# Attention and a two-layer network in one kernel: the last eight token blocks taken in pairs, with seven half-size products for the first layer

## The chip, the cores and the metric

The kernel runs on one core of a Trainium2 chip. Its engines are TensorE (matrix products, with separate weight loads), VectorE (DVE in the profile), ScalarE (ACT), GpSimd (POOL) and SyncE (SP), whose queue issues the transfers (DMA). TensorE writes its products into PSUM, eight banks of 512 float32 values on each of 128 partitions; VectorE and ScalarE read them from there. The metric is device time in microseconds of one execution, as the median of the runs.

## The reference

A linear attention is followed by a two-layer network over its output. For 8 batches and 8 heads, with 576 positions of 64 values and 128 features:

```
proj = x @ w_phi;  proj -= max(abs(proj), last axis)
phi(x) = concat(exp(proj), exp(-proj))              # 256 features, of q and of k
kv = phi(k)^T @ v;   z = sum over positions of phi(k)
attn = (phi(q) @ kv) / (phi(q) @ z + 1e-6)
x = attn as 4608 tokens of 512 values
h = x @ w_in                 # 512 -> 2048
out = gelu(h) @ w_out        # 2048 -> 512, gelu with erf
```

## The kernel before

Attention is worked batch by batch (`attention`, `k_quad`, `q_pair`, `quotients`): projections and sums on TensorE (tiles pk, kv, pq, pn), exponentials on ScalarE, maxima and denominators across partitions on GpSimd (mb, db). Numerators go to DRAM as x_d, reciprocal denominators as r_d. The 64-bit weights are turned into float32 once at the start (`split_weight`).

The network takes 18 blocks of 256 tokens. Every factor is held as two parts, the value rounded to TensorE's fast 32-bit form (float32r) and the remainder, and a product is three matmuls: high x high, high x low, low x high. `tokens` loads a block's numerators (xr) and reciprocals, multiplies and splits them (xh, xl). `up` computes a 128-feature part of the first layer into a PSUM tile ph, with 12 matmuls of 128 x 256 (four chunks of the 512 inputs, times three). Each block has eight units u with two such parts, so 192 matmuls.

Blocks 0 to 7 (`block`) run while attention is still under way: gelu on ScalarE, the remainder on VectorE, second layer into tile po with 96 matmuls of 128 x 512. Blocks 8 to 17 (`seven`) run after it. There the second layer of a unit is a 2 x 2 product of halves, in Strassen's way: seven products (m1 to m7) of sums of halves instead of eight, 21 matmuls of 128 x 256 into a four-bank tile pm. Sums of the activations (sg, oh, ol, uh, ul) are made on VectorE and ScalarE, sums of the second layer's weights once, during blocks 2 to 5 of the plan (`sums_of_weights`, tiles ts), stored in DRAM (t_d) and fetched back at block 8 into tw and over parts of w_o (`fetch_sums`). `turn_over` then closes attention's pools and reopens their space. Each later block is 192 + 168 = 360 matmuls of 256 columns.

The order of work is not written by hand. Each operation is recorded with engine, cost, rank, buffers and dependences (`Plan.op`); `Plan.order` runs a list schedule with these costs and ranks, a model of transfers among them, and `emit` writes every engine's instructions in that order. Engines, and SP's queue, then work strictly through their lists, and an instruction that waits holds up all behind it. The constants at the end of the file set ranks, delays (`since`) and lumps of attention work on TensorE (`LUMP`, `LINGER`). Line 329 is the helper `mm` for all matmuls, 364 to 370 are the helpers `copy` and `tt`, so groups are told apart by tiles.

## Time and profile before

| what | value |
|---|---|
| median of 3 runs (lowest to highest) | 1088.41 us (1087.9 to 1089.75) |
| the profiled execution | 1087.47 us |
| its span, first to last instruction | 1085.7 us |
| mean granted TensorE clock | 0.991 |
| moved by DMA | 106.05 MB |

The profile is of one execution. The page gives busy time by engine, the chain of work that ended last, and groups of instructions; other views give stretches of time, groups kept apart by shape, and every instruction in order. Matmuls overlap: a matmul of 256 columns is listed with some 0.28 us, and the next one starts 0.113 us after it. So the time of TensorE's work is read from starts, not from durations. The same holds on VectorE, where an instruction's duration overlaps the start of the next. In a row of a group, the last part is the idle time of the engine before these instructions and what ended it.

### The profile page before, as it was taken

The page shows a single profiled execution, that of the slowest core. Times are in us where ns is not written, and L with a number is a line of the kernel's source. Part 1 is how long each engine was busy: PE and PEld are TensorE (multiplying, and loading weights), DVE is VectorE, ACT ScalarE, POOL GpSimd, SP SyncE. Part 2 cuts the span into 40 slices and gives each one's busy share as a digit, 9 for nine tenths or more (in the row PEclk, how much of TensorE's full clock was granted, in tenths as well). Part 3 has the DMA queues.
Part 4 walks back from the last instruction along what each step waited for, and adds up shares of the span by engine and source line. Part 5 has one row for each costly group of instructions (what it writes and reads, how often), then busy time and mean ns, then how long its engine had stood idle before and what let it go on. Part 6 is the DMA issues. An engine that isn't in the chain of part 4 may idle for free.

```text
span 1085.7 us, 24204 instructions
## 1 busy us (share of the span) xinstructions
PE 1052.7 (97%) x9857; PEld 915.4 (84%) x9857; DVE 701.4 (65%) x1323; ACT 642.2 (59%) x1083; POOL 325.7 (30%) x116
## 2 busy tenths in 40 slices
PE   7879999999999999999999999999999999999996
PEld 4547858887877788877788888999999999999996
DVE  5888989467879997775653444465465465466444
ACT  5768786786767777766677683344344343344333
POOL 1321225754635755557655561000000000000000
PEclk8999999999999999999999999999999999999998
DMA  6887532224343343432321336421021021021000
GB/s 251 261 244 221 180 86 87 62 87 140 101 147 109 113 148 111 133 107 59 94 71 30 102 89 203 170 59 40 20 59 40 21 59 40 21 59 39 2 21 21
DMA packets 85216, 106.05 MB, mean 98 GB/s; under 512 B 24992, under 2 KB 66112, under 8 KB 85104
## 3 DMA queue, kind: packets, MB, share of 16 engines
q1 hardware_dynamic: 85104, 104.50, 31.6%
q8 instruction: 77, 1.26, 0.5%
q14 instruction: 35, 0.29, 0.1%
HBM read 74.81 MB, written 29.66 MB: 96 GB/s over the span
## 4 chain that ended last, share of the span: by engine, by line
PE 78%; DVE 11%; ACT 4%; DMA 3%; issue 2%; POOL 1%; SPq 0%; ACTq 0%; DVEq 0%; POOLq 0%
PE ph L329 33%; PE pm L329 18%; PE po L329 13%; PE kv L329 4%; PE pn L329 4%; PE pq L329 2%; PE pk L329 2%; DVE ts L370 2%; ACT ek L459 1%; DVE mx L454 1%; DVE ek L370 1%; DMA x_d<-xo 1%; DVE pc L370 1%; POOL db L537 1%; DVE un L531 1%
## 5 line engine op out<-in xcount | busy, mean ns | idle before, releaser
L329 PE MATMUL ph<-xh,w_i 128*128 128x256 f32 x2304 | 418.6, 278 | 1.1 <-ACT ga L714 0.7
L329 PEld LDWEIGHTS ph<-xh,w_i 128*128 128x128 f32 x2304 | 357.3, 188 | 8.2 <-issue 4.8
L329 PE MATMUL ph<-xl,w_i 128*128 128x256 f32 x1152 | 318.6, 277 | 0.0
L537 POOL PARTITION_ALL_REDUCE db<-un x48 | 182.1, 3793 | 159.7 <-DVE un L534 152.2
L329 PEld LDWEIGHTS ph<-xl,w_i 128*128 128x128 f32 x1152 | 216.4, 188 | 0.3
L502 POOL PARTITION_ALL_REDUCE mb<-pc x64 | 145.7, 2276 | 174.6 <-ACT pc L364 133.2
L370 DVE TENSOR_TENSOR sg<-ga 128x256 f32<-128x256 f32 (+1 forms) x240 | 84.5, 376 | 160.8 <-ACT ga L714 157.9
L329 PE MATMUL po<-w_o,gh 128*128 128x512 f32 (+1 forms) x520 | 164.8, 399 | 0.0
L714 ACT ACTIVATE ga<-ph 128x512 f32<-128x512 f32 x80 | 47.7, 597 | 165.6 <-PE ph L329 161.9
L329 PEld LDWEIGHTS po<-w_o,gh 128*128 128x128 f32 x520 | 92.5, 188 | 26.6 <-issue 4.7
L329 PE MATMUL pm<-w_o,oh 128*128 128x256 f32 x640 | 114.0, 277 | 0.0
L329 PEld LDWEIGHTS kv<-vt,ek 128*64 128x64 f32 (+1 forms) x2560 | 84.8, 140 | 27.2 <-issue 13.0
L329 PE MATMUL pn<-ef,kvn 128*64 128x288 f32 (+1 forms) x512 | 96.6, 422 | 7.9 <-ACT xo L364 7.7
L329 PE MATMUL po<-w_o,gl 128*128 128x512 f32 (+1 forms) x289 | 101.1, 368 | 0.4 <-DVE gl L370 0.4
L459 ACT ACTIVATE ek<-ek 128x1024 f32<-128x1024 f32 (+1 forms) x96 | 80.8, 843 | 32.7 <-DVE ek L370 31.6
L329 PEld LDWEIGHTS pm<-w_o,oh 128*128 128x128 f32 x640 | 96.5, 188 | 0.2 <-issue 0.2
L329 PE MATMUL kv<-vt,ek 128*64 128x65 f32 (+1 forms) x2560 | 93.7, 227 | 3.0 <-ACT ek L459 2.3
L508 ACT ACTIVATE ef<-pc 128x576 f32<-128x576 f32 x128 | 81.6, 678 | 14.7 <-DVE pc L370 14.2
L329 PE MATMUL pm<-w_o,ol 128*128 128x256 f32 x320 | 88.5, 277 | 0.0
L329 PE MATMUL pm<-tw,uh 128*128 128x256 f32 x480 | 86.0, 277 | 0.0
L370 DVE TENSOR_TENSOR pc<-pc,mb 128x576 f32<-128x576 f32 x64 | 50.9, 795 | 44.0 <-POOL mb L502 44.0
L370 DVE TENSOR_TENSOR gl<-ph,gh 128x512 fp32r<-128x512 f32 x64 | 43.8, 685 | 49.8 <-ACT ph L633 43.4
(63 smaller groups left out, 1549.7 us busy)
## 6 DMA issues: line engine op xcount, KB each, us to landing
t_d<-ts SPq DMA_DIRECT2D x40, 256.0 KB
vt<-in_va_dram SPq DMA_DIRECT2D x16, 585.0 KB
qt<-in_qT_dram SPq DMA_DIRECT2D x64, 144.0 KB
kt<-in_kT_dram SPq DMA_DIRECT2D x16, 576.0 KB
out_dram<-ob SPq DMA_DIRECT2D x36, 256.0 KB
raw_i<-in_w_in_dram SPq DMA_DIRECT2D x16, 512.0 KB
raw_o<-in_w_out_dram SPq DMA_DIRECT2D x16, 512.0 KB
x_d<-xo SPq DMA_DIRECT2D x48, 144.0 KB
```

Source lines behind the costliest of these rows:

```text
L329: return tc.keep_in_program_order(nc.tensor.matmul(*a, **kw))
L370: op(eng, cost, lambda: e.tensor_tensor(out=dst(), in0=a(), in1=b(), op=o), r=r, w=w, **kw)
L454: op("dve", dve(256 * n, True), lambda xs=xs, mx=mx: nc.vector.tensor_reduce(out=mx(), in_=xs(), axis=AX.X, op=ALU.max, apply_absolute_val ...
L459: op("act", act(256 * n), lambda e=e, s=s: nc.scalar.activation(e[s](), e[1](), AF.Exp, scale=1.0 - 2.0 * s), r=[e[1]], w=[e[s]], table="e ...
L502: op("pool", 2.2, lambda mb=mb, pc=pc: nc.gpsimd.partition_all_reduce(mb(), pc(), P, bass_isa.ReduceOp.absmax), r=[pc], w=[mb], port="max" ...
L508: op("act", act(2 * HS), lambda ef=ef, pc=pc, s=s: nc.scalar.activation(ef()[:, s], pc(), AF.Exp, scale=1.0 - 2.0 * s), r=[pc], w=[ef], ta ...
L531: op("dve", dve(HS, fast=True) + 0.06, lambda un=un, ef=ef, one=one, j=j: nc.vector.tensor_scalar(out=un()[:, j], in0=ef()[:, 0, j], scala ...
L537: op("pool", 3.7, lambda db=db, un=un: nc.gpsimd.partition_all_reduce(db(), un(), P, bass_isa.ReduceOp.add), r=[un], w=[db], port="add", * ...
L714: op("act", act(2 * TB, True) + 0.037, lambda ph=ph, ga=ga: nc.scalar.activation(ga(), ph(), AF.Gelu), r=[ph_all], w=[ga], table="gelu", **dr)
```

## The change

Blocks 8 and 9 stay single (`single`). Blocks 10 to 17 are taken two at a time (`pair`): the 512 tokens x 512 inputs of a pair and the weights of features u and u + 8 are each taken as 2 x 2 halves, and the first layer of a unit becomes seven products of half size (Winograd's form of Strassen's scheme), each of six matmuls of 128 x 256, instead of two blocks' 2 x 24 matmuls. Their sums of tokens (b11, t1 to t4, b21, b22) are formed once for a pair (`pair_tokens`); sums of w_in are formed during the early blocks, stored in DRAM (m_d) together with the plain parts, and read again for each pair through a ring of four slots (ri), which lie where the no longer needed w_in parts were. The seven products of a unit go in turn to the halves of two PSUM banks (ph twice, or h0 and h1), from where ScalarE and VectorE gather them: a running sum s, the first block's activations ga and the second block's gb. gb is kept until the first block's second layer is done (`seconds` runs first for block j, then for block j + 1). The running sum s and the first quarter of the result (c11) share space in a corner of former weights.

The second layer's accumulators, one tile pm of four banks before, become pa0, pa1 (one bank each) and pb; `results` and `single` combine them in another order.

Sums of weights are now made from whole values: high and low part are added once for each weight tile (`whole`), then sums and differences are formed, rounded and given their remainders (`rounded`). Before, each sum added both parts of both weights and then the two halves. The planner's constants are all different, and attention's pace is a constant of its own (`AT`). Shortened, the diff reads:

```diff
-    EARLIER = dict(kt=2, vt=2, mx=2, ek=2, kvn=4, un=1, db=1, qt=2, pc=2, mb=1, ef=2, xo=2, dc=2)
+    EARLIER = dict(kt=2, vt=2, mx=2, ek=2, kvn=4, un=1, db=1, qt=2, pc=2, mb=1, ef=2, xo=2, dc=2, wr=1, ws=1)
...
-    LATER = dict(ga=1, sg=1, uh=2, ul=2) | {f"tw{k}": 1 for k in range(NFC // 2)}
+    LATER = {f"tw{k}": 1 for k in range(NFC // 2)} | {f"xo{k}": 1 for k in range(3)} | dict(xe=1)
...
-        t: plan.pool(lambda: shared[1], t, n) for t, n in dict(pp=1, kv=1, pn=1, pm=1).items()}
+        t: plan.pool(lambda: shared[1], t, n) for t, n in dict(pp=1, kv=1, pn=1, pa0=1, pa1=1, h0=1, h1=1).items()}
...
+    def rounded(plain, src, rank, places):
+        kw = dict(rank=rank)
+        t = sb["ob"]([P, 2, HDM], F32R, f"ts_{next(rounds)}")
+        copy("act", act(HDM), lambda: t()[:, 1], plain, [src], [t], **kw)
+        tt("dve", dve(HDM), lambda: t()[:, 0], plain, lambda: t()[:, 1].bitcast(F32), ALU.subtract, [src, t], [t], **kw)
...
+    def whole(dst, buf, w, cols, n, rank):
+        tt("dve", dve(n), dst, lambda: w().bitcast(F32)[:, 0, cols], lambda: w().bitcast(F32)[:, 1, cols], ALU.add, [w], [buf], rank=rank)
...
-            for i, (x, xc, y, yc, o) in enumerate((
-                    (b, low_cols, a, high_cols, ALU.add), (b, low_cols, b, high_cols, ALU.add), (a, low_cols, a, high_cols, ALU.add),
-                    (b, high_cols, a, high_cols, ALU.subtract), (a, low_cols, b, low_cols, ALU.subtract))):
...
-                tt("dve", dve(2 * HDM), plain, lambda x=x, xc=xc: x().bitcast(F32)[:, :, xc], lambda y=y, yc=yc: y().bitcast(F32)[:, :, yc], o, [x, y], [t], **kw)
-                tt("dve", dve(HDM), lambda low=low: low().bitcast(F32), lambda low=low: low().bitcast(F32), lambda high=high: high().bitcast(F32), ALU.add, [t], [t], **kw)
-                copy("act", act(HDM), high, lambda low=low: low().bitcast(F32), [t], [t], **kw)
-                tt("dve", dve(HDM), low, lambda low=low: low().bitcast(F32), lambda high=high: high().bitcast(F32), ALU.subtract, [t], [t], **kw)
...
+            for i, w in enumerate((wo[k], wo[k + 8])):
+                whole(lambda raw=raw, i=i: raw()[:, 2 * i : 2 * i + 2].rearrange("p a t -> p (a t)"), raw, w, slice(0, DM), DM, rk)
...
+            for i, dst, buf, x, y, o in ((0, new(0), sum_, bl, ar, ALU.add), (1, new(1), sum_, bl, br, ALU.add), (3, br, raw, br, ar, ALU.subtract),
+                                         (2, ar, raw, al, ar, ALU.add), (4, al, raw, al, bl, ALU.subtract)):
+                tt("dve", dve(HDM), dst, x, y, o, [raw], [buf], rank=rk)
+                rounded(dst, buf, rk, [(d, lambda d=d, i=i: d()[:, i], lambda p: p)])
+        first = [Buf(plan, None, lambda e=e: dpool.tile([P, 2, 2, 2, P], F32, name=f"m_d{e}")) for e in range(7 * NFC // 4)]
...
+                    quarters = a11, a21, a12, a22 = wi[ci, q], wi[ci, q + 2], wi[2 + ci, q], wi[2 + ci, q + 2]
...
+                    for i, w in enumerate(quarters):
+                        whole(one(i), raw, w, cols, HDM, rk)
...
+                    for pos, dst, x, y, o in ((2, r22, r21, r22, ALU.add), (3, r21, r11, r21, ALU.subtract), (1, r11, r22, r11, ALU.subtract), (4, r12, r12, r11, ALU.subtract)):
+                        tt("dve", dve(HDM), dst, x, y, o, [raw], [raw], rank=rk)
...
+                        rounded(dst, raw, rk, places)
+                    for x, pos in ((a11, 0), (a22, 5), (a12, 6)):
...
+        xb = slot("w_i3_2", [P, NCC, TB], F32, f"xr_{j + 1}")
+        factor = slot("w_i0_2", [P, NCC, TB], F32, f"rb_{j}")
...
+        scaled_tokens(j, xa, factor, URGE + rank - SOON)
+        scaled_tokens(j + 1, xb, factor, URGE + rank - SOON)
+        half = lambda t, k: (lambda: t()[:, 2 * k : 2 * k + 2])
+        tt("dve", cost, half(factor, 0), half(xb, 1), half(xb, 0), ALU.subtract, [xb, factor], [factor], **soon)
+        tt("dve", cost, half(xb, 0), half(xb, 0), half(xa, 0), ALU.subtract, [xa, xb], [xb], **soon)
+        tt("dve", cost, half(factor, 1), half(xb, 1), half(xb, 0), ALU.subtract, [xb, factor], [factor], **soon)
+        X = {}
+        for k, tag, src, buf in (("b11", "xh", half(xa, 0), xa), ("t2", "xl", half(factor, 1), factor), ("t1", "xo0", half(xb, 0), xb),
+                                 ("t3", "xo1", half(factor, 0), factor), ("b22", "xo2", half(xb, 1), xb), ("t4", "xh", None, None), ("b21", "xl", half(xa, 1), xa)):
+            x = X[k] = sb[tag]([P, 2, 2, TB], F32R, f"x{k}_{j}")
+            hi, lo = (lambda x=x: x()[:, 0]), (lambda x=x: x()[:, 1])
+            if k == "t4":
+                tt("dve", cost, half(factor, 1), half(xa, 1), half(factor, 1), ALU.subtract, [xa, factor], [factor], **rk)
+                src, buf = half(factor, 1), factor
+            late = dict(after=after) if tag[:2] == "xo" else {}
+            copy("act", act(2 * TB), hi, src, [buf], [x], **late, **rk)
+            tt("dve", cost, lo, src, lambda hi=hi: hi().bitcast(F32), ALU.subtract, [buf, x], [x], **rk)
...
+    RING = [f"w_i{c}_0" for c in range(4)]
...
+            taken.update(hold=hold, more=more, s=sub(hold, 512, 768, "p (o t) -> p o t", o=1), c11=sub(hold, 768, 1024, "p (o t) -> p o t", o=1),
...
+        tt("dve", dve(2 * P), lambda: df()[:, 0:2], lambda: g()[:, :, P:], lambda: g()[:, :, :P], ALU.subtract, [ga], [df], **dr)
+        tt("dve", dve(P), lambda: df()[:, 2], quarter(2), quarter(1), ALU.add, [ga], [df], **dr)
+        copy("act", act(3 * P), uh, df, [df], [uh], **dr)
+        tt("dve", dve(P), quarter(0), quarter(0), quarter(2), ALU.add, [ga], [ga], **dr)
+        tt("dve", dve(P), quarter(3), quarter(3), quarter(1), ALU.add, [ga], [ga], **dr)
+        copy("act", act(2 * P), lambda: oh()[:, 2:4], ends, [ga], [oh], **dr)
+        tt("dve", dve(2 * P), flat(ol, 0, 2), mid, f32(flat(oh, 0, 2)), ALU.subtract, [ga, oh], [ol], **dr)
+        tt("dve", dve(3 * P), ul, df, f32(uh), ALU.subtract, [df, uh], [ul], **dr)
+        tt("dve", dve(2 * P), lambda: ol()[:, 2:4], ends, lambda: oh()[:, 2:4].bitcast(F32), ALU.subtract, [ga, oh], [ol], **dr)
...
+    def accumulators(j):
+        pa0, pa1 = (ps[t]([P, DM], F32, f"{t}_{j}") for t in ("pa0", "pa1"))
+        pb = ps["po"]([P, 2, DM], F32, f"pb_{j}")
+        return pa0, pa1, pb, dict(m4=lambda: pa0()[:, left], m5=lambda: pa0()[:, right], m3=lambda: pa1()[:, left], m2=lambda: pa1()[:, right],
+                                      m7=lambda: pb()[:, 0, left], m6=lambda: pb()[:, 0, right], m1=lambda: pb()[:, 1, left])
...
+        copy("act", act(DM, True), o0, pa0, [pa0], [o0], **kw)
+        copy("act", act(DM, True), o1, pa1, [pa1], [o1], **kw)
...
+        tt("dve", dve(HDM), one, m4, m5, ALU.subtract, [o0], [one_buf], **kw)
+        tt("dve", dve(HDM, True), one, one, part["m7"], ALU.subtract, [one_buf, pb], [one_buf], port=False, **kw)
...
+        for m, h, src, t in ((0, right, c12, o0), (1, left, c21, o0), (0, left, one, one_buf), (1, right, c22, o1)):
...
-        pm = ps["pm"]([P, 4, DM], F32, f"pm_{j}")
...
+    def pair(j, tw, first, rank, after):
+        X = pair_tokens(j, rank(0) - 4, after)
...
+        for e in range(7 * NU // 2):
+            n_ring = (j - PAIRED) // 2 * 28 + e
+            t = slot(RING[n_ring % len(RING)], [P, 2, 2, 2, P], F32R, f"ri_{j}_{e}")
+            ring.append(t)
+            op("sp", 0.06, lambda t=t, e=e: nc.sync.dma_start(out=t().bitcast(F32), in_=first[e]()), r=[first[e]], w=[t], kb=524, rank=rank(PHASE * e / 28) - 20)
...
+        for u in range(NU):
+            rk = rank(PHASE * u / NU)
+            banks = [ps[t]([P, 2, TB], F32, f"ph_{j}_{u}_{k}") for k, t in enumerate(("ph", "ph") if u % 2 == 0 else ("h0", "h1"))]
...
+            ga, s = z[f"ga{u % 2}"], z[("s", "c11")[u % 2]]
...
+                def go():
+                    ins = []
+                    for ci in range(2):
+                        for w, x in ((0, 0), (0, 1), (1, 0)):
+                            ins.append(mm(banks[k]()[:, half, :], lhsT=ring[e]()[:, side, ci, w ^ swap, :], rhs=X[xb]()[:, x, ci, :],
+                                          start=pos < 2 and not ins, stop=len(ins) == 5, skip_group_check=True))
...
+            product(0, 0, "b11", 0)
+            copy("act", act(TB, True), s, whole(banks[0], 0), [banks[0]], [s], **dr)
+            product(1, 1, "t2", 0)
+            add(s, s, s, [s], 1, 0)
+            product(2, 0, "t1", 1)
+            add(whole(gb, 1), gb, s, [s], 0, 1)
+            product(3, 1, "t3", 1)
+            add(whole(gb, 1), gb, whole(gb, 1), [gb], 1, 1)
+            product(4, 0, "b22", 1)
+            add(whole(gb, 0), gb, s, [s], 0, 1)
+            product(5, 1, "t4", 1)
+            add(whole(ga, 1), ga, s, [s], 1, 1)
+            product(6, 0, "b21", 0)
+            op("act", act(TB, True) + 0.037, lambda ga=ga, banks=banks: nc.scalar.activation(ga()[:, 0, :], banks[0]()[:, 0, :], AF.Gelu), r=[banks[0]], w=[ga], table="gelu", **dr)
+            op("act", act(TB) + 0.037, lambda ga=ga: nc.scalar.activation(ga()[:, 1, :], ga()[:, 1, :], AF.Gelu), r=[ga], w=[ga], table="gelu", **dr)
+            op("act", act(2 * TB) + 0.037, lambda gb=gb: nc.scalar.activation(gb(), gb(), AF.Gelu), r=[gb], w=[gb], table="gelu", **dr)
+            seconds(j, u, ga, ga, tw, state, rank(PHASE * (u + LAG) / NU), [z["hold"], z["more"]])
+            later.append((gb, gb_all))
+        results(j, state, rank(PHASE))
+        state = accumulators(j + 1)
+        for u in range(NU):
+            gb, gb_all = later[u]
+            seconds(j + 1, u, gb, gb, tw, state, rank(PHASE + (1 - PHASE) * u / NU), [gb_all])
+        results(j + 1, state, rank(1))
...
+        if j < PAIRED:
+            single(j, tw, lambda x, t=t, d=d: t + d * x, earlier)
+        elif (j - PAIRED) % 2 == 0:
+            pair(j, tw, first, lambda x, t=t, d=d: t + 2 * d * x, earlier)
...
@@ -794,35 +1044,46 @@
 
 
 SEVEN = 8
+PAIRED = 10
+PHASE = 0.51
...
...
```

308 lines of the change are left out of this document (225 added, 83 removed).

## The prediction

> **What bounds the kernel now.** I read the page first (busy shares, the chain), then the stretches, then the groups of the last stretch.
>
> ```profile
> span 1085.7 us, 24204 instructions
> PE 1052.7 (97%) x9857; PEld 915.4 (84%) x9857; DVE 701.4 (65%) x1323; ACT 642.2 (59%) x1083; POOL 325.7 (30%) x116
> PEclk8999999999999999999999999999999999999998
> PE 78%; DVE 11%; ACT 4%; DMA 3%; issue 2%; POOL 1%; SPq 0%; ACTq 0%; DVEq 0%; POOLq 0%
> ```
>
> TensorE is busy 97% of the span at the full granted clock, and the chain that ends last is 78% TensorE. The stretches (start:end and length, then busy us with instruction counts for PE, PEld, DVE, ACT, POOL, then clock, DMA share, GB/s) say where this holds:
>
> ```profile
> 0.00:54.00 54.00, 42.61 (x524) 28.11 (x526) 35.81 (x56) 34.96 (x59) 15.24 (x11) 0.94 0.75 257
> 54.00:108.00 54.00, 47.16 (x439) 31.27 (x436) 46.38 (x73) 39.88 (x73) 11.42 (x5) 0.94 0.80 234
> 324.00:432.00 108.00, 106.94 (x1037) 86.11 (x1038) 97.25 (x149) 81.64 (x124) 65.38 (x22) 1.00 0.39 119
> 432.00:540.00 108.00, 108.00 (x1082) 87.03 (x1083) 69.44 (x112) 72.13 (x112) 66.80 (x24) 1.00 0.33 99
> 540.00:660.00 120.00, 120.00 (x1056) 98.40 (x1055) 56.20 (x96) 87.16 (x121) 66.38 (x23) 1.00 0.28 77
> 840.00:900.00 60.00, 60.00 (x530) 59.98 (x529) 34.56 (x88) 24.21 (x51) 0.00 (x0) 1.00 0.14 36
> ```
>
> Only the first 108 us leave TensorE idle, 18 us of them. After attention, whose last products start at 661.48 us (first row below), TensorE has no gap, VectorE works 34.6 of 60 us and DMA 14%. A product taken out there shortens the span by its own issue time, as long as nothing new makes TensorE wait. The chain in order of time gives that issue time (start, us, what):
>
> ```profile
> 661.48 1.12 PE pn L329 x8
> 751.69 5.45 PE ph L329 x48
> 761.24 4.76 PE pm L329 x42
> ```
>
> 48 products of 256 columns take 5.45 us, 42 take 4.76: 0.1133 us each, for both layers.
>
> **The change, part by part.** *First products.* Two blocks of 256 tokens cost 2 x 192 = 384 such products; a pair costs 8 units x 7 x 6 = 336. Over four pairs 192 go: 192 x 0.1133 = **-21.8 us**. All stand in the stretch without gaps, so all count. Second products keep number and shape.
>
> *Handoffs inside a pair.* Where a block's unit filled one PSUM tile with 24 products while another tile was read, the seven products of a unit now go in turn onto two banks, and each of the products 2 to 6 may start only when the last product on its bank has been read by ScalarE or VectorE: 5 x 8 x 4 = 160 handoffs. TensorE, block 17 before (the sum of the first layer, then second products):
>
> ```order
> L329 MATMUL ph_6_12879<-xh_11976,w_i_1_1006 128x256
> L329 MATMUL ph_6_12879<-xl_12122,w_i_1_1006 128x256
> L329 MATMUL ph_6_12879<-xh_11976,w_i_1_1006 128x256
> L329 MATMUL pm_12647<-w_o_1130,oh_5_12861 128x256 x2
> L329 MATMUL pm_12647<-w_o_1130,ol_5_12876 128x256
> ```
>
> and the same engine where the pair of blocks 14 and 15 begins (ph_14_u_k is bank k of unit u, xt and xb its token sums, ri_14_e the ring of weights):
>
> ```order
> L330 MATMUL pb_13_11287<-tw_7_8002,uu_13_7_11461 128x256 x3
> L330 MATMUL ph_14_0_1_11172<-xt3_14_11049,ri_14_1_11031 128x256 x6
> L330 MATMUL ph_14_0_0_11148<-xb22_14_11061,ri_14_2_11059 128x256 x6
> L330 MATMUL ph_14_0_1_11172<-xt4_14_11215,ri_14_2_11059 128x256 x6
> L330 MATMUL ph_14_0_0_11148<-xb21_14_11101,ri_14_3_11088 128x256 x6
> L330 MATMUL ph_14_1_0_11184<-xt1_14_11034,ri_14_4_11192 128x256 x6
> L330 MATMUL ph_14_1_1_11276<-xt3_14_11049,ri_14_5_11537 128x256 x6
> L330 MATMUL ph_14_1_0_11184<-xb22_14_11061,ri_14_5_11537 128x256 x6
> L330 MATMUL ph_14_1_1_11276<-xt4_14_11215,ri_14_6_11561 128x256 x6
> L330 MATMUL pb_14_11617<-tw_0_7982,uu_14_0_11585 128x256 x6
> ```
>
> Here a bank comes back after one other product of six. Over all pairs the order has 35 such tight handoffs, 18 with nine products between, and 107 with twelve or more. What a handoff needs stands in the groups by form after 700 us and in the tail:
>
> ```profile
> L370 DVE TENSOR_TENSOR ob<-ob,pm 128x256 f32<-128x256 f32 x40 | 14.6, 415 | 0.6 <-ACT ob L364 0.6
> 1077.90 0.28 PE L329 MATMUL pm<-tw,ul 128*128 128x256 f32 x1
> 1078.21 1.07 ACT L364 COPY ob<-pm 128x512 f32<-128x512 f32 x2 [2.22 <-PE pm L329]
> 1079.31 2.61 DVE L370 TENSOR_TENSOR ob<-ob,pm 128x512 f32<-128x512 f32 x6 [2.74 <-ACT ob L364]
> 1081.62 0.81 SPq L759 DMA_DIRECT2D out_dram<-ob  x2
> ```
>
> A product's last matmul ends 0.28 us after its start, the reader starts 0.03 later (1078.18 to 1078.21, 1079.28 to 1079.31), VectorE's read of 256 PSUM columns takes 0.415; with 0.03 for the way back, which no row shows, 0.76 us. The other bank's product gives 7 x 0.1133 = 0.79 from that same start. So a tight handoff fits if VectorE is free, and not otherwise. How busy VectorE is follows from rows of one unit of block 11:
>
> ```profile
> 810.40 0.76 DVE L370 TENSOR_TENSOR sg<-ga 128x256 f32<-128x256 f32 x2 [5.89 <-ACT ga L714]
> 811.08 0.42 DVE L370 TENSOR_TENSOR ol<-ga,oh 128x256 fp32r<-128x256 f32 x1
> 811.41 0.29 DVE L370 TENSOR_TENSOR sg<-ga 128x128 f32<-128x128 f32 x1
> 811.62 0.42 DVE L370 TENSOR_TENSOR ol<-sg,oh 128x256 fp32r<-128x256 f32 x1
> 812.28 0.56 DVE L370 TENSOR_TENSOR ul<-sg,uh 128x384 fp32r<-128x384 f32 x1 [0.24 <-ACT uh L364]
> L370 DVE TENSOR_TENSOR ob<-ob,pm 128x512 f32<-128x512 f32 x20 | 13.1, 684 | 11.0 <-ACT ob L364 11.0
> L370 DVE TENSOR_TENSOR xr<-xr,xh 128x1024 f32<-128x1024 f32 x8 | 9.8, 1220 | 0.3 <-DMA xh<-r_d 0.2
> ```
>
> From start to start 256 columns take 0.34 us and 128 take 0.21; a row overlaps the next by some 0.08, so 384 take 0.48, 512 take 0.60, 1024 take 1.14. A pair has, per unit, five PSUM additions (1.7) and two preparations of second operands of 3 x 0.34 + 3 x 0.21 + 0.48 = 2.13: 8 x 5.96 = 47.7; tokens 2 x 1.14 + 11 x 0.60 = 8.9; results 16 x 0.34 = 5.4. Together 62 us beside 672 x 0.1133 = 76.1 us of TensorE: 81%, where now it is 58%. A tight handoff meets a busy VectorE with chance 0.8 and waits half of a 0.34 operation: 35 x 0.8 x 0.17 = **+4.8 us**. From below 0 (the list puts these reads in their places); from above each tight one waits for a whole 0.56 and each with nine products 0.3: 25. I take 4.8, which lies nearer the rows of a free VectorE. [...]
>
> *Where a pair begins.* Output rows of the pair before, its freed buffers and the ring meet on SP's queue. SP, last blocks before:
>
> ```order
> L595 DMA xr_17_11651<-x_d7_3_1_7758 128x256
> L599 DMA xh_17_11976<-r_d7_1_7780 64x4x256 x2
> L759 DMA out_0_dram<-ob_15_0_12057 128x512
> L759 DMA out_0_dram<-ob_15_1_12062 128x512
> L759 DMA out_0_dram<-ob_16_0_12602 128x512
> ```
>
> and SP now, where blocks 14 and 15 begin:
>
> ```order
> L755 DMA rb_16_11326<-r_d7_1_7951 64x4x256 x2
> L954 DMA ri_14_5_11537<-m_d5_5276 128x1024
> L883 DMA out_0_dram<-corner3_9176 128x256
> L883 DMA out_0_dram<-ob_13_0_11515 128x256 x2
> L954 DMA ri_14_6_11561<-m_d6_4941 128x1024
> L954 DMA ri_14_7_11566<-m_d7_5865 128x1024
> ```
>
> The loads ri_14_6 and ri_14_7 now stand behind three output transfers that wait for block 13's results. Also, unit 1 keeps its running sum in the corner buffer that block 13's first output is read from, so ScalarE's copy there waits for that transfer to land. Call T the start of block 13's last matmul. Two copies (0.5 each, overlapping its end) and four VectorE operations put the transfer's issue at about T + 2.0. Its time to landing is at most 1085.7 - 1081.6 = 4.1 us (the tail row above, two transfers, to the span's end) and at least the 0.8 of issuing. With 3.3 and 0.3 of copying, unit 1's product xt1 starts at T + 5.6, where the products before it alone would let it start at T + (1 + 4 x 6) x 0.1133 = T + 2.8: 2.8 us lost. The waits for the ring run beside it. Pairs 14 and 16 begin so; 10 and 12 have other work between: 2 x 2.8 = **+5.6 us**, from 0 to 10 (3.6 at two starts, 1.2 at the two others).
>
> *The ring.* 28 loads of 512 KB for a pair, each 14 first products. The load of the second layer's sums shows what DMA can do beside full TensorE:
>
> ```profile
> 675.00:680.00 5.00, 1.00 1.01 415
> 678.69 5.44 PE ph L329 x48
> ```
>
> 415 GB/s is 1.26 us a load, against 12 x 0.1133 = 1.36 us of first products alone and 2.0 with the second ones between; TensorE held its 0.1133 at that load. Hidden, but for the starts above. [...]
>
> *Sums of weights.* These stand under attention, where VectorE operations last longer (groups by form, 200 to 640 us):
>
> ```profile
> L370 DVE TENSOR_TENSOR ts<-ts 128x256 fp32r<-128x256 f32 x40 | 28.9, 722 | 8.2 <-ACT ts L364 8.1
> L370 DVE TENSOR_TENSOR ts<-ts 128x256 f32<-128x256 f32 x40 | 23.7, 593 | 0.4
> L370 DVE TENSOR_TENSOR ts<-w_o,w_o 128x512 f32<-128x512 f32 x24 | 21.0, 874 | 0.3 <-DMA t_d<-ts 0.3
> L370 DVE TENSOR_TENSOR ts<-w_o 128x512 f32<-128x512 f32 x16 | 13.8, 863 | 1.2 <-DMA t_d<-ts 1.2
> ```
>
> Now 87.4 us. After: 16 x 0.87 + 104 x 0.593 + 72 x 0.722 = 127.6, so +40. The order spreads them to block 7 where they ended with block 6; from 432 to 660 us VectorE is idle 102 us, and the first reader comes after attention. Zero; without that cover up to 40.
>
> *Attention.* It is pulled forward by 204 product times, which are paid later, and TensorE changes between layers and attention 92 times instead of 83:
>
> ```profile
> 653.01 0.28 PE L329 MATMUL ph<-xh,w_i 128*128 128x256 f32 x1
> 653.22 1.19 PE L329 MATMUL pn<-ef,kvn 128*64 128x288 f32 x8
> 654.34 0.74 PE L329 MATMUL po<-w_o,gh 128*128 128x512 f32 x2
> 655.15 0.62 PE L329 MATMUL po<-w_o,gh 128*128 128x512 f32 x2
> ```
>
> 0.21 - 0.11 going in and 0.74 - 0.62 coming out: 9 x 0.22 = **+2.0 us**. The reordered start can move the 18 us of idle time either way; -5 to +8, taken as 0. The tail is as long as before within 1 us: results read two finished accumulators early, but the last products have less work beside them.
>
> **Sum**: 1085.7 - 21.8 + 4.8 + 5.6 + 2.0 = 1076.3 us of span. The profiled execution took 1087.47 us (1.8 around the span), the median is 0.9 above it: 1076.3 + 2.7 = **1079.0 us**.
>
> **Rivals.** *Nothing waits*: handoffs and starts are covered by the list, the reordered start gains a little: 1085.7 - 21.8 + 2 + 2.7 = 1068.6, less up to 5. For it: 107 wide handoffs; against: 81% on an engine that works in order. *The front grows*: VectorE at 97 of 108 us between 324 and 432 cannot take its part of the 40, and a fifth of it, 8 us, reaches TensorE: 1087. Against it, 102 idle us behind. *The handoff decides*: late reads on VectorE hold up the next product, whose lateness delays the next read. With 0.17 us at each of the 160 it is 27 instead of 4.8: 1101, **slower**; it decides from (21.8 - 5.6 - 2.0) / 160 = 0.09 us each.
>
> **How the numbers follow.** Forecast (1071 to 1085) 0.60; nothing waits 0.18; the front 0.11; the handoff 0.11. Range 1065 to 1089, which leaves out the worst of the handoffs and of the front. About 0.2% (2.2 us) is what a measurement can tell. The front's 1087 lies on the edge of that. Faster: 0.60 + 0.18 + 0.05 = 0.83; same 0.06; slower 0.11.
>
> **What would show it.** Right: 3264 first products, 0.1133 each, after attention; TensorE idle in pairs some 10 us, ended by VectorE and ScalarE reads of ph; VectorE near 80%. Wrong: idle time at every handoff, TensorE waiting for ri in mid-pair, or a last attention product later than 645 us.

## The result and the profile after

The changed kernel takes 1102.66 us (median of four runs, 1099.69 to 1107.39) against 1089.08 us of the kernel before beside it: ratio 1.013, 95% interval 1.0084 to 1.0175. It is **slower**; 1079.0 us was forecast. The profiled execution took 1099.69 us, 12.2 us more than the one before; it is the fastest of the four, 3 us below their median, so what follows accounts for 12.2 us.

The page of the changed kernel: span, busy shares, granted clock by fortieths, and the chain that ended last.

```profile
span 1097.9 us, 24764 instructions
PE 1048.1 (95%) x9648; PEld 901.3 (82%) x9648; DVE 812.1 (74%) x1683; ACT 675.7 (62%) x1223; POOL 322.2 (29%) x116
PEclk8998999999999999999999999999999999999999
PE 41%; DVE 4%; DMA 3%; ACT 1%; issue 1%; SPq 0%; DVEq 0%; ACTq 0%
```

TensorE has 209 matmuls fewer (192 products of 256 columns, if one of 512 counts as two) and is busy 4.6 us less in a span that is 12.2 us longer. I split both traces at the start of the last attention product. Stretches of the kernel before (start:end and length, busy us with counts for PE, PEld, DVE, ACT, POOL, then clock, DMA share, GB/s):

```profile
0.00:662.20 662.20, 637.52 (x6232) 501.59 (x6232) 474.44 (x753) 478.12 (x738) 325.69 (x116) 0.99 0.41 126
662.20:1078.02 415.82, 415.04 (x3629) 413.81 (x3625) 224.31 (x564) 163.04 (x343) 0.00 (x0) 1.00 0.18 53
```

and of the changed kernel:

```profile
0.00:652.05 652.05, 619.55 (x6069) 482.71 (x6069) 505.76 (x815) 480.14 (x760) 317.66 (x115) 0.98 0.50 147
652.05:1092.55 440.50, 428.43 (x3583) 418.58 (x3579) 303.94 (x862) 195.55 (x464) 4.57 (x2) 1.00 0.60 189
```

Behind that point stand 3636 products of 256 columns before, counted in the same way, and 3648 after: at 0.1133 us, 412.0 of 415.8 us before, and 413.3 of 440.5 us after. A stretch without gaps has become one in which TensorE waits a sixteenth of the time.

For a finer count I take, for every matmul, the time from its start to the next one's start, less the step that its shape has when nothing holds it (medians of the trace before: 0.1133 us for 256 columns of the network, 0.231 for 512, and so for attention's shapes). The sum of what is left is called **waiting** here; half clock counts into it. **Front** is the waiting up to the last attention product, with the 2.3 us ahead of the first matmul; **behind** is the waiting after it.

| profiled execution | steps of all products | front | behind | last start to end | span |
|---|---|---|---|---|---|
| before | 985.2 | 89.0 | 3.7 | 7.8 | 1085.7 |
| after | 963.4 | 102.2 | 26.8 | 5.5 | 1097.9 |
| difference | -21.8 | +13.2 | +23.1 | -2.3 | +12.2 |

So the products' gain is there in full and is paid back twice: 13 us in front of the pairs, 23 us in them.

In the front the changed kernel (the first two rows answer to rows of the prediction):

```profile
0.00:54.00 54.00, 42.52 (x514) 28.06 (x516) 34.17 (x53) 34.13 (x58) 13.06 (x10) 0.91 0.78 258
54.00:108.00 54.00, 46.40 (x424) 30.20 (x421) 43.90 (x68) 39.74 (x71) 14.05 (x7) 0.90 0.71 203
108.00:216.00 108.00, 100.36 (x1014) 76.87 (x1012) 101.86 (x155) 84.25 (x135) 43.02 (x16) 0.98 0.40 118
```

and the kernel before in the third of these stretches:

```profile
108.00:216.00 108.00, 103.98 (x1065) 81.50 (x1065) 88.93 (x145) 82.14 (x133) 46.90 (x16) 1.00 0.35 104
```

The granted clock fell from 0.94, 0.94 and 1.00 to 0.91, 0.90 and 0.98. 54 x 0.19 + 108 x 0.02 = 12.4 us of full clock are missing instead of 6.5: up to 6 of the 13 us are TensorE at half clock. The clock record shows half clock (0.5) in pieces of 3.41 us or multiples of it, here for one from 163.99 us on, behind 3.5 us in which TensorE was busy for 0.98. The place and number of these pieces differ between the two traced executions of the changed kernel: behind the last attention product the first has none, the second one of 3.41 us.

In the pairs, what instructions that write or read ph waited for (us in total, times; all engines together):

```profile
  PE ph L330: 61.9, 108
  ACT corner L365: 8.6, 6
  DMA out_dram<-corner: 5.5, 3
  DMA ri<-m_d: 5.2, 8
  DVE uu L371: 3.6, 3
  DVE corner L371: 2.3, 5
```

The first row is ScalarE and VectorE waiting for products, which costs nothing. The others are engines held ahead of a product or of its reader, TensorE among them. Two places where TensorE waits (start, us, what, and in brackets the idle time before it and what ended it):

```profile
864.71 1.56 PE L330 MATMUL ph<-xt,ri 128*128 128x256 f32 x11 [1.32 <-DMA ri<-m_d]
939.86 0.37 ACT L365 COPY corner<-ph 128x256 f32<-128x256 f32 x1 [1.10 <-DMA out_dram<-corner]
940.28 0.97 PE L330 MATMUL ph<-xt,ri 128*128 128x256 f32 x6 [2.69 <-ACT corner L365]
```

At 864.71, in mid-pair, TensorE waits for a load of the ring. At 940.28, where blocks 14 and 15 begin, it waits for ScalarE's copy into the corner, which waits for the output transfer of block 13 out of that corner. Single waits over 0.15 us make up 17 of the 27 us, 4.5 of them ended by loads of the ring; the rest is many small ones.

### The profile page after: what moved, and what is told of

Its sections match the earlier page's. It is cut to its first block, busy times and chain, and to the rows that moved or that the text cites. A ratio compares the mean times of both kernels' runs of the same rounds, so it can differ in the third digit from the quotient of the medians.

```text
span 1097.9 us, 24764 instructions
## 1 busy us (share of the span) xinstructions
PE 1048.1 (95%) x9648; PEld 901.3 (82%) x9648; DVE 812.1 (74%) x1683; ACT 675.7 (62%) x1223; POOL 322.2 (29%) x116
## 4 chain that ended last, share of the span: by engine, by line
PE 41%; DVE 4%; DMA 3%; ACT 1%; issue 1%; SPq 0%; DVEq 0%; ACTq 0%
PE ph L330 19%; PE pa L330 8%; PE pb L330 6%; PE po L330 4%; DMA ri<-m_d 2%; PE pn L330 1%; DVE corner L371 1%; PE kv L330 1%; DMA out_dram<-corner 1%; DVE ob L371 1%; PE pq L330 0%; DVE xr L371 0%; PE pk L330 0%; DVE uu L371 0%; ACT ob L365 0%
## 5 line engine op out<-in xcount | busy, mean ns | idle before, releaser
L330 PE MATMUL ph<-xh,w_i 128*128 128x256 f32 x1280 | 239.3, 282 | 1.2 <-DVE gl L371 1.2
L330 PEld LDWEIGHTS ph<-xh,w_i 128*128 128x128 f32 x1280 | 199.9, 188 | 12.5 <-issue 7.8
L330 PE MATMUL ph<-xl,w_i 128*128 128x256 f32 x640 | 177.5, 277 | 0.0
L330 PEld LDWEIGHTS ph<-xl,w_i 128*128 128x128 f32 x640 | 120.3, 188 | 0.2
L330 PE MATMUL ph<-xt,ri 128*128 128x256 f32 x768 | 106.6, 281 | 8.8 <-ACT corner L365 2.7
L330 PEld LDWEIGHTS ph<-xt,ri 128*128 128x128 f32 x768 | 95.7, 188 | 12.1 <-ACT corner L365 3.2
L330 PE MATMUL po<-w_o,gl 128*128 128x512 f32 (+1 forms) x276 | 101.1, 378 | 0.8 <-DVE gl L371 0.8
L330 PE MATMUL pa<-w_o,oh 128*128 128x256 f32 x472 | 84.3, 277 | 0.0
L330 PE MATMUL ph<-xb,ri 128*128 128x256 f32 x576 | 80.2, 281 | 1.2 <-DMA ri<-m_d 1.0
L330 PE MATMUL pb<-tw,uu 128*128 128x256 f32 x576 | 79.5, 279 | 1.8 <-DVE ob L371 1.3
L330 PEld LDWEIGHTS pb<-tw,uu 128*128 128x128 f32 x576 | 71.7, 188 | 3.2 <-DVE ob L371 2.1
```

The lines of the kernel that those rows point to most:

```text
L330: return tc.keep_in_program_order(nc.tensor.matmul(*a, **kw))
```

## The experiments

Numbers of each run are in the table at the end of this section; front and behind are of its one profiled execution, the time is the median. Two executions of the changed kernel itself have 26.8 and 30.3 us behind, so 3 us behind, between single executions, settle nothing. The kernel before took 1088.0 to 1088.7 us beside all of them.

**The front: constants or sums?** First the changed kernel with the fourteen old constants of the front and the old pace of attention, and the kernel before with the new ones (the same lines the other way round):

```diff
-T15 = 833.0
+T15 = 897.27
...
-T0 = 97.23
-AT = 86
+T0 = 109.39
+AT = (897.27 - 109.39) / 7
```

> The changed kernel with the planner's constants of the kernel before for the front (ranks, delays and lumps of attention and weights), the sums and the pairs as changed. Up to the last attention product the changed kernel lost 13 us: 652 us less 2832 network products of 0.1133 is 331, before 662 less 3036 of them is 318. The theory that the new constants cost this (more and shorter attention stretches, TensorE idle long enough for its clock to be halved) expects 318 again: here 3120 network products stand ahead of the last attention product, so it starts at about 672 us, and the span falls by 13 to about 1085. The theory that the added sums of first-layer weights on VectorE cost it expects the 331 to stay: last attention at about 684 us, span about 1098.

> The kernel before with the new front constants and nothing else. If the constants cost the 13 us, the last attention product starts at about 331 + 2784 x 0.1133 = 646 us and the span is 13 longer than before, about 1099. If the added sums cost it, 318 + 315 = 633 us and a span of about 1086.

and the changed kernel in which the ring's weights are the plain parts, so that no sum of w_in is formed:

```diff
-    tt("dve", dve(HDM), dst, x, y, o, [raw], [raw], rank=rk)
-    rounded(dst, raw, rk, places)
+    for (d, where, _), u in zip(places, us):
+        op("sp", 0.06, lambda where=where, w=quarters[pos - 1], u=u: nc.sync.dma_start(
+            out=where(), in_=w().bitcast(F32)[:, :, u % 4 * P : u % 4 * P + P]), r=[quarters[pos - 1]], w=[d], kb=131, rank=rk)
```

> The changed kernel with the new constants, but the sums of first-layer weights are not formed: plain parts are stored in their places, so 64 additions, 32 roundings on ScalarE and 32 remainders on VectorE are left out (some 60 us of VectorE's busy time), and the outputs of the last eight blocks are not the reference's. Transfers keep their sizes. If the added sums cost the 13 us of the front, the last attention product starts at about 639 instead of 652 us and the span is about 1085; if the constants do, both stay within 4 us (652, 1098).

All three missed. The front took 111.5, 112.1 and 112.9 us: each program's front is 9 or 23 us worse with the other's constants, and taking work away from the changed kernel without setting its constants anew made its front 11 us *longer*. A part of it is half clock: by the clock records up to 5.1 of the 9.3 us, 13.7 of the 23.1 and 5.1 of the 10.7. A front's time in these runs is not a sum of its parts; it belongs to the whole order that the list schedule makes of them.

**Small changes of the order.** One constant each, of the kernel before and then of the changed one:

```diff
-SUMSEACH = 5.81
+SUMSEACH = 6.11
...
-SUMSAT = 213.95
+SUMSAT = 214.95
```

> The kernel before with one constant of its order changed: the sums of w_out may begin 6.11 us apart instead of 5.81 us. Every instruction is the same, 259 of the 932 groups of products on TensorE stand at another place in its order, and the order written out by hand puts its own end 2.6 us later than the one it replaces. Theory 1 (the front's time belongs to the whole fixed order, how much slack each wait and the clock have in it, and not to the work in it): 1092 to 1100, with TensorE's waiting in front of the last attention product up by 4 to 10 us from 89. Theory 2 (the +13 us in front of the changed kernel come from its new work there, the sums of w_in and larger buffers): 1088.5 plus or minus 2, since no work is added.

> The changed kernel with one constant of its order changed: the sums of w_out may begin at 214.95 instead of 213.95 us. Every instruction is the same, 408 of the 1188 groups of products stand at another place in TensorE's order, and the order by hand puts its own end 1.1 us later. Theory 1 (the front's time belongs to the fixed order): it differs from the changed kernel by 2 to 10 us in either direction, in the front and not behind the last attention product. Theory 2 (the front pays for its work): the same as the changed kernel, 1100 to 1107, front 102 plus or minus 2.

The changed kernel lost 9.9 us (1112.5), its front 113.6:

```profile
0.00:668.80 668.80, 628.69 (x6103) 487.87 (x6104) 508.23 (x819) 483.95 (x764) 317.86 (x115) 0.98 0.48 144
```

The kernel before lost 1.3 us (ratio 1.0012, 1.0000 to 1.0023), less than I expected of theory 1. So an order of the same work can cost 10 us, and need not. Against this stands how well one order repeats: the eight other profiled executions below that keep the changed kernel's front have 100.1 to 102.7 us there.

**What the sums of w_in cost.** They are added to the kernel before, where nobody reads them, and then with their stores cut to one value per partition (`first_sums` is the second half of the changed kernel's `sums_of_weights`, with a group each 16 us):

```diff
+            first_sums(lambda x: FIRST + FIRSTSPAN * x)
...
-    out=where(), in_=part(t().bitcast(F32))
+    out=where()[:, 0, :1], in_=part(t().bitcast(F32))[:, 0, :1]
```

> The kernel before, which also forms and stores the changed kernel's sums of w_in under attention (VectorE, ScalarE and 112 transfers to DRAM as in the changed kernel); nobody reads them, all else is the kernel before with its constants. They may begin at 397 us, one group each 16 us, a place where the order by hand puts its own end only 0.3 us later than the kernel before's. Theory W (the front's +13 us is the work of these sums): TensorE's waiting in front of the last attention product 97 to 103 instead of 89, time 1096 to 1102. Theory O (the +13 us is the fixed order that the changed kernel got with its new constants; the sums fit into idle time): 88 to 94 and 1088 to 1093.

> The run that added the sums of w_in to the kernel before, in the same order, with each of their 112 stores cut to one value per partition, so that the sums are formed on VectorE and ScalarE but 14.7 MB less is moved under attention. That run took 1091.3 us against 1088.0 of the kernel before. If the 3.4 us are the transfers: 1087.5 to 1089. If they are the work of VectorE and ScalarE, or the changed order: 1090.5 to 1092.5.

1091.3 us, ratio 1.0036 (1.0023 to 1.0050): +3.4 us, in theory O's range, with a front of 95.7 us in the profiled execution, the slowest of the four. With the stores cut it is 1092.5 (ratio 1.0033, 1.0021 to 1.0044), the same: it isn't the transfers but VectorE's and ScalarE's work, or the order with it, which these runs don't separate. Then the changed kernel with the old front, the old way to form w_out's sums, and the sums of w_in spread like this:

```diff
-LASTEACH = 1.65
+LASTEACH = 4
-T15 = 833.0
+T15 = 845.0
...
-T0 = 97.23
-AT = 86
+T0 = 109.39
+AT = (897.27 - 109.39) / 7
```

> The changed kernel with the front of the kernel before: its constants, its way of forming the sums of w_out (no sums from whole values there), and the sums of w_in spread as in the run before this one (one group each 16 us). Blocks 8 to 17 are as in the changed kernel. Theory O (fixed order): front 88 to 95 instead of 102, waiting behind the last attention product 24 to 29 as in the changed kernel, time 1084 to 1092. Theory W (the sums of w_in cost the front): front 98 or more, time 1095 or more.

1096.0 us, more than theory O allowed, but not by the front; the two stretches are

```profile
0.00:664.00 664.00, 634.90 (x6198) 497.77 (x6200) 523.48 (x848) 475.21 (x760) 328.06 (x116) 0.99 0.49 148
664.00:1088.90 424.90, 410.02 (x3461) 402.07 (x3457) 299.48 (x853) 193.65 (x460) 1.68 (x1) 1.00 0.59 191
```

with 95.0 us of front (95.7 in the kernel before with the sums). So of the profiled +13 us, 3.4 (by the medians of the kernel before with and without them) to 6 (by single executions) go with the sums of w_in, and the other 7 to 10 with the new order or the new way to form w_out's sums, which no run separates. It stays slower than the kernel before, since the pairs (30.3) still cost more than they save.

**The pairs: VectorE, SyncE's queue, or the ring?** Three edits of the changed kernel. Without the remainders of the second operands (ol and ul aren't formed, the products take the rounded parts in their place):

```diff
-    tt("dve", dve(2 * P), flat(ol, 0, 2), mid, f32(flat(oh, 0, 2)), ALU.subtract, [ga, oh], [ol], **dr)
-    tt("dve", dve(3 * P), ul, df, f32(uh), ALU.subtract, [df, uh], [ul], **dr)
...
```

> The changed kernel with the remainders of the second layer's operands left out in the pairs (three of seven VectorE operations of each preparation, 1.16 us of 2.13); TensorE reads the rounded parts in their place, so every product is still issued and the outputs of the last eight blocks differ in the last digits. VectorE's load in a pair falls from 81% to some 57%. If VectorE's load makes TensorE wait in the pairs (24 us beyond its issue time between 756 us and its last product, against 3 before), this falls below 9 and the span to about 1082. If the handoffs cost by themselves, by the way from engine to engine, or if transfers do, it stays near 24 and the span near 1098.

```profile
651.10:1089.40 438.30, 426.42 (x3583) 418.12 (x3579) 233.92 (x670) 193.77 (x464) 4.61 (x2) 1.00 0.59 190
```

VectorE falls from 303.9 to 233.9 us behind the last attention product, and TensorE's waiting only from 26.8 to 24.6. That speaks against VectorE's load as what holds the pairs. It does not exclude it: from 776 us on, in the first pair, TensorE's products stand in an order made anew, and another order alone can cost as much as was hoped for here. Next the output transfers on GpSimd's queue:

```diff
-    (nc.scalar if eng == "act" else nc.sync).dma_start(
+    (nc.scalar if eng == "act" else nc.gpsimd).dma_start(
```

> The changed kernel with the output transfers of the pairs issued on GpSimd's queue instead of SyncE's, so that no load of weights or tokens stands behind an output transfer that waits for VectorE. Theory A (loads of the ring are late because they stand behind outputs in SyncE's queue): the waits of the pairs that end on the loads (4.5 us) and the 2.85 us at the start of the pair of blocks 14 and 15 go, waiting behind the last attention product 18 to 21 instead of 26.8, time 1094 to 1099. Theory B (loads are late because four tiles are too few for the rate of the transfers, and the corner's wait is for its transfer wherever it is issued): 25 to 29 us, time 1100 to 1107.

It got worse, 1109.4 us and 32.0 behind, which neither theory had. TensorE's order is the changed kernel's up to 943 us, and up to there the waiting behind is 21.6 us against 21.1: loads behind outputs in SyncE's queue are not the cause. What is worse is half clock where pairs begin, 10.2 us of it by the clock record, at 938.96 and 1024.29 us; that is up to 5.1 us of full clock, as much as the difference:

```profile
1022.00:1032.00 10.00, 7.08 (x38) 6.88 (x37) 2.11 (x5) 1.24 (x3) 0.24 (x1) 0.66 0.50 166
```

Then no loads of the ring after the first four:

```diff
+    if n_ring >= len(RING):
+        ring.append(kept[e % len(RING)])
+        continue
```

> The changed kernel without the loads that bring the half-size first weights back in the pairs: only the first four are loaded and every product then reads one of these four tiles, so the values are not the reference's; instructions of all engines stay, 108 transfers of 512 KB and the waits on them go. The front's order is the same. Theory A (the ring of four tiles is what the pairs wait for, directly and because VectorE, ScalarE and the PSUM banks start late behind it): of the 26.8 us that TensorE waits behind the last attention product 10 to 14 go, span 1084 to 1088, time 1087 to 1094 with the changed kernel at 1100 to 1107. Theory B (only the waits that end on these loads, 4.5 us, go; the rest are reads of PSUM banks): 4 to 6 us, waiting 21 to 23, time 1095 to 1101.

```profile
651.30:1077.40 426.10, 423.78 (x3583) 418.31 (x3579) 299.77 (x862) 195.68 (x465) 4.62 (x2) 1.00 0.20 62
```

1082.8 us, faster than the kernel before (ratio 0.9948, 0.9928 to 0.9967), though it leaves out 108 of 112 loads, so that its results are of no use; behind 12.3 instead of 26.8. Theory A held, with a little more than its 10 to 14: **14.5 us of the pairs' loss go with the ring**, three times the 4.5 us of waits that end on a load.

**Why the ring costs it.** In this run the order of the pairs is another too, made for no loads. The next two keep the changed kernel's order, queues, tiles and waits to the last instruction, and make each load smaller, 256 KB or 64 KB (the products then read the part that was loaded); the third has 256 KB and an order made for it:

```diff
-    nc.sync.dma_start(out=t().bitcast(F32), in_=first[e]())
+    nc.sync.dma_start(out=t().bitcast(F32)[:, 0], in_=first[e]()[:, 0])
...
+    nc.sync.dma_start(out=t().bitcast(F32)[:, 0, 0, 0], in_=first[e]()[:, 0, 0, 0])
...
-    kb=524
+    kb=262
```

> The changed kernel in the same order, with the same loads of the ring, queues and waits, but each load after the first four brings 256 KB instead of 512 KB, and both products of a load read this half, so the values are not the reference's. Theory R (the loads come too late because 512 KB take too long beside what else moves: some 1.9 us at the 276 to 287 GB/s of the pairs' first halves): waiting behind the last attention product 12 to 17 instead of 26.8, as without the ring, time 1083 to 1089. Theory D (the loads come too late because four tiles are freed too late, or stand behind waits in SyncE's queue, whatever their size): 21 to 27, time 1094 to 1106.

> As the run with 256 KB loads, in the order of the changed kernel, but each load after the first four brings 64 KB, which all products of the load read, so the values are not the reference's. With 256 KB TensorE waited 19.7 us behind the last attention product, no more for a load, against 26.8 with 512 KB and 12.3 with no loads and an order made without them. If the 7 us between are still the time of the loads: 12 to 15, time 1083 to 1087. If they are the order, which was made for loads that come late and keeps its distances when they come early: 18 to 21, time 1089 to 1093.

> The run with 256 KB loads, with the order of the pairs made anew for loads of that size (its own list puts the end only 0.6 us earlier). If the last 7 us of the ring are the order's distances: 12 to 16 behind the last attention product, time 1083 to 1088. If a new order for half-size loads gives nothing, as the list says: 18 to 22, time 1089 to 1094.

The stretches behind the last attention product, one row of each kernel in this order:

```profile
649.80:1083.30 433.50, 427.44 (x3583) 418.23 (x3579) 303.34 (x862) 195.41 (x464) 4.58 (x2) 1.00 0.40 126
```

```profile
651.90:1085.50 433.60, 427.37 (x3583) 418.02 (x3579) 303.42 (x862) 195.54 (x465) 4.61 (x2) 1.00 0.26 77
```

```profile
651.90:1094.70 442.80, 429.85 (x3583) 422.01 (x3579) 302.24 (x862) 195.42 (x464) 4.57 (x2) 0.99 0.39 124
```

Waiting 19.7, 19.8 and 29.0. With half the bytes no wait ends on a load any more, and with an eighth nothing further is won: the bytes of the loads are worth **7.1 us** (11.4 in the medians, 1102.7 to 1091.3). 19.7 lies between the ranges of both theories, and the run with 64 KB came out on the side on which the bytes no longer count.

The remaining 7.4 us, from 19.7 to 12.3, came back only in the run without loads. That run has another order of the pairs, but it also takes 108 loads and their waits for free tiles out of SyncE's queue, so it is not shown whose these 7.4 us are. The order made for 256 KB, with the same bytes as the first, is 9.3 us worse than the old one, which I had in neither range. It is no proof that an order costs by itself, for here TensorE waits for loads again:

```profile
  DMA ri<-m_d: 4.9, 5
777.85 0.93 PE L330 MATMUL ph<-xt,ri 128*128 128x256 f32 x6 [2.21 <-DMA ri<-m_d]
```

The second row is the longest of them. Counted from starts, as waiting is above, these five waits are 5.8 us, and two pieces of half clock in the first pair take up to 3.4 us: together about the 9.3. So what this order costs is late loads once more, and the clock with them.

How close the loads of 512 KB run shows in stretches of the changed kernel, two first halves of pairs and a second half:

```profile
870.00:905.00 35.00, 34.30 (x290) 33.70 (x289) 26.32 (x69) 17.91 (x42) 0.00 (x0) 1.00 0.87 276
940.00:980.00 40.00, 39.72 (x343) 39.54 (x344) 27.57 (x78) 18.43 (x45) 0.00 (x0) 1.00 0.88 287
980.00:1022.00 42.00, 41.51 (x362) 41.14 (x361) 36.90 (x110) 21.39 (x50) 0.00 (x0) 1.00 0.39 124
```

These 276 to 287 GB/s are what the pairs ask for, not what DMA can do. SyncE issues a load when its tile comes free (in most places 0.03 us after the last product that reads it has ended), so the loads follow the pace of their use, some 2.0 us each (ten and 21 loads in a row, start and length in us), and with 256 KB a load the same stretch moves half as much:

```profile
886.74 17.96 SPq L954 DMA_DIRECT2D ri<-m_d  x10
941.28 37.43 SPq L954 DMA_DIRECT2D ri<-m_d  x21
870.00:905.00 35.00, 35.00 (x306) 34.96 (x305) 28.19 (x79) 19.21 (x46) 0.00 (x0) 1.00 0.45 145
```

At full DMA share the same traffic would run at some 320 GB/s (an estimate, 276 / 0.87 and 287 / 0.88), 1.6 us a load where the prediction had 1.26 (415 GB/s). And a load is long under way. With packet records of 4096 bytes taken in order, 128 to a load, and products in order, 12 matmuls to a load, I estimate 4.0 to 4.5 us from its issue to the end of its last packet, in the median of such stretches, and up to 6 in the pairs; its first product stands 5.3 to 7.4 us behind its issue. So DMA is nearly full while the first products run, half idle while the second ones do, and a load that takes a little longer than usual is late.

**Can it be won back?** Three more tiles for the ring (places of the second block's gates that are still empty), alone and with the old front, the second time also with the pairs' constants set anew, and those once more:

```diff
+    MORE = {4: 'w_i2_1', 5: 'w_i1_1', 6: 'w_i3_1'}
-            t = slot(RING[n_ring % len(RING)], [P, 2, 2, 2, P], F32R, f"ri_{j}_{e}")
+            t = slot(MORE[e] if e in MORE else RING[next(turns) % len(RING)], [P, 2, 2, 2, P], F32R, f"ri_{j}_{e}")
...
-PHASE = 0.51
+PHASE = 0.478
...
-LAG = 5.08
+LAG = 3.766
...
-SOON = 25.91
+SOON = 57.685
```

> The changed kernel with one edit: in each pair the fifth, sixth and seventh load of the ring go to the tiles in which the gates of the second block will stand from the third, fifth and seventh step on, so that seven loads instead of four can be there before a pair begins. Theory A (the pairs' waits come from too few loads ahead): waiting behind the last attention product 20 to 24 instead of 26.8, time 3 to 6 us under the changed kernel's 1100 to 1107. Theory C (loads of 512 KB come as fast as the transfers run, and a few more ahead do not help in the long first half of a pair): 25 to 28, time 1100 to 1107.

> The last two together, with eight of the constants that order the pairs set anew. Theory O and A: front 88 to 95, behind it 18 to 23, time 1078 to 1086 and so faster than the kernel before (1088.4). Theory C: 1084 to 1092, no different from the run with the old front.

> The run with the old front and more tiles for the ring, with ten constants of the pairs' order set once more (products of a pair begin earlier, sums of w_in 18.6 us apart from 445 us on). That run took 1093.0 us. If what is left behind the last attention product (24.5 us) is a matter of the order within the pairs: 1084 to 1089, faster than the kernel before or the same. If it is the rate of the loads and the chain over VectorE and ScalarE that any order meets: 1090 to 1095.

1096.9, 1093.0 and 1091.7 us: each step gains some, the second less than expected, and the best is still 0.34% (0.21 to 0.48) slower than the kernel before; no order that was tried makes the change pay. Of more_ring the time fell by 6 us, while its profiled execution, the slowest of its four, shows 28.0 behind; up to 3.4 us of that are half clock (6.83 us from 765.93 us on), which the first execution of the changed kernel has not got behind, and without it 24.6 would be left. The last two have the same 3.4 us in theirs.

Since the changed kernel's own runs lie apart, it was run once more.

> The changed kernel itself, run again, since its four runs lie apart (1099.7, 1099.8, 1105.5, 1107.4) and the experiments' differences are read against it. If the upper two belong to it: median 1100 to 1106 again. If they were single disturbances: 1098 to 1101.

1103.2 us (1101.1 to 1105.0). The profiled one of these, 1101.9 us of span, shows where the two traced executions differ (TensorE at the start of the first pair):

```profile
773.62 0.84 PE L330 MATMUL ph<-xb,ri 128*128 128x256 f32 x6
777.40 0.95 PE L330 MATMUL ph<-xt,ri 128*128 128x256 f32 x6 [2.93 <-DMA ri<-m_d]
778.18 1.09 PE L330 MATMUL ph<-xb,ri 128*128 128x256 f32 x6
```

```profile
778.00:783.00 5.00, 5.00 (x32) 5.00 (x32) 2.32 (x8) 2.19 (x6) 0.00 (x0) 0.66 0.85 305
```

A wait of 2.93 us for a load, and from 778.65 us TensorE runs at half clock for 3.41 us: 32 matmuls in 5 us. In the first profiled execution the same 5 us had 47, at clock 1.00. In the 3.41 us before, TensorE had stood still for 2.16. Here the late load cost a second time: the clock fell after it, which is up to 1.7 us.

The last column but one is half of the time that the clock record has at half clock behind the last attention product, which is the most that it can have cost.

| run | time us | front | behind | of it half clock | what it shows |
|---|---|---|---|---|---|
| before | 1088.4 | 89.0 | 3.7 | 0 | |
| after | 1102.7 | 102.2 | 26.8 | 0 | |
| after_again | 1103.2 | 102.7 | 30.3 | 1.7 | half clock at the first pair |
| old_constants | 1128.2 | 111.5 | 44.4 | 8.5 | an order made with other constants |
| before_new_constants | 1112.1 | 112.1 | 5.0 | 0 | the same, other way |
| no_first_sums | 1112.8 | 112.9 | 33.4 | 3.4 | less work, worse order |
| before_nudged | 1089.6 | 93.4 | 4.0 | 0 | a small change need not cost |
| after_nudged | 1112.5 | 113.6 | 28.5 | 0 | a small change can |
| before_plus_sums | 1091.3 | 95.7 | 4.5 | 0 | sums of w_in: +3.4 |
| sums_small_stores | 1092.5 | 91.8 | 4.3 | 0 | not their transfers |
| old_front | 1096.0 | 95.0 | 30.3 | 1.7 | front -7 |
| pairs_light | 1096.8 | 101.4 | 24.6 | 0 | against VectorE's load, order made anew |
| outputs_on_gpsimd | 1109.4 | 101.5 | 32.0 | 5.1 | not the outputs in SyncE's queue |
| no_ring | 1082.8 | 101.6 | 12.3 | 0 | ring: 14.5 |
| half_ring | 1091.3 | 100.1 | 19.7 | 0 | of it 7.1 the loads' bytes |
| eighth_ring | 1092.5 | 102.2 | 19.8 | 0 | no more below 256 KB |
| half_ring_replanned | 1102.9 | 102.2 | 29.0 | 3.4 | waits for loads again |
| more_ring | 1096.9 | 101.1 | 28.0 | 3.4 | |
| old_front_more_ring | 1093.0 | 97.6 | 24.5 | 3.4 | |
| retuned | 1091.7 | 97.0 | 24.0 | 3.4 | best of the pairs, not faster than before |

## Why the prediction was wrong, step by step

**First products, -21.8 us: right.** The steps of all products fell from 985.2 to 963.4 us. This largest term held.

**The ring, "hidden, but for the starts above": this step failed.** I took the rate of one load of the second layer's sums, 415 GB/s over 5 us, for 28 loads in a row beside everything else, got 1.26 us against 2.0 us of use, and put the ring at nothing. The loads did keep the pace of use; what was wrong is that this hides them. By the estimate above a load took 4.0 to 4.5 us to arrive, up to 6, three to five times the 1.26 us of that rate, and its tile comes free only 5.3 to 7.4 us before it is needed again. The measured price is 14.5 us: 7.1 that go with the bytes of the loads, and 7.4 more that go only when the loads go, which the runs do not take apart. (The prediction's "each 14 first products" is a slip: a load serves two products, 12 matmuls, and its sum uses 12.) The trace of the pairs stays a third below the 415, at 276 GB/s and a DMA share of 0.87, at the pace of use. "TensorE waiting for ri in mid-pair" stood among the signs that would show me wrong, and came.

**Handoffs +4.8 and starts +5.6: right in kind, and together near in size.** Without the ring, 12.3 - 3.7 = 8.6 us of new waiting remain in the pairs, 6.8 of them in pieces under 0.15 us, against 10.4 forecast. The start's wait at the corner is not among them; it shows in the changed kernel, and of the two forecast only that of blocks 14 and 15: TensorE stood 2.69 us there, in the way described, where 2.8 was said. VectorE's load was as forecast, 258 of 336.6 us from the start of the pairs to TensorE's last product, 77% where 81% was said:

```profile
756.00:1092.55 336.55, 324.48 (x2740) 317.71 (x2738) 258.14 (x733) 157.27 (x372) 0.00 (x0) 1.00 0.64 202
```

That this load sets the price of the handoffs did not show: 70 us less of VectorE's work, in an order made anew, took 2.2 us away. With the bytes of the loads (7.1) the forecast would have come to 1086 and with the ring's other 7.4 to 1093.5, past the kernel before.

**The front, "taken as 0", from -5 to +8: this step failed too, with its upper bound.** It measured +13.2, with the changes between layers and attention (forecast +2.0) in it. The bounds had been set by the 18 us of idle time at the start and by VectorE's idle time under attention, as if moved work cost only what it displaces. Busy shares were the wrong measure for them: counted from starts, 89 us of the front were waiting before the change already, and it is these that a new order moves. The sums of w_in on VectorE are 122.9 us long with those of w_out (forecast 127.6), and fit, but the kernel before pays 3.4 us for them too (6 in single executions); the other 7 to 10 us go with an order made anew, or with the new way to form w_out's sums. This step alone would have carried the forecast to 1090 (1079 + 13.2 - 2.0), so either of the two was enough to turn the sign. The last attention product stood at 652.0 us, later than the 645 that I had named as the sign.

**The tail, 0:** 2.3 us shorter.

Sum by these terms: -21.8 + 23.1 + 13.2 - 2.3 = +12.2, the difference of the two spans. Of the rivals, "the front grows" named the direction, with 8 of 13 us, but its reason, VectorE's work on the sums, is worth 3.4 to 6. "The handoff decides" gave 1101, close to the measured time, but that is luck: without the ring no such price was left. Among the signs, "3264 first products after attention" counts those of all 18 blocks; 1728 belong to blocks 8 to 17.

What stays open: whether the ring's other 7.4 us are the order's or the loads' places in SyncE's queue (with 256 KB TensorE has two dozen waits over 0.15 us, none for a load and all but two for VectorE or ScalarE; without the ring it has five), whether VectorE's or ScalarE's share of the sums costs the 3.4 us, and what of the front is the new way to form w_out's sums.

## What to carry to other kernels

Where a schedule fixed beforehand fills TensorE to 97%, price a change as a new order and not as a sum of edits: the same instructions in another order moved this kernel by 1 to 10 us, and a removed piece of work can make it slower until its constants are set anew. Set the bounds of such a term from waiting counted by starts, not from busy shares. Where resident weights become a stream, a rate that keeps up with the use does not yet hide the loads (here they kept the 2.0 us of their use and cost 14.5 us): compare the time from a load's issue to its arrival, at the place where it will run and with all that moves beside it, with the time from the release of a tile to its next use. And before calling a stretch's GB/s a limit, see whether it is only what was asked for: with half the bytes a load it halved (276 GB/s to 145).
